# Search of sub-keys laid over 44 attention steps instead of 33, with a new buffer layout and later key and value loads

## The chip, the cores and the metric

One core of a Trainium2 chip runs the whole kernel. The time is the device time of one execution in microseconds (us). TensorE (PE in the profile) does the matrix products, ScalarE (ACT) the exponentials and the copies with a scale, VectorE (DVE) the searches for maxima and the element-wise work, GpSimd (POOL) the rest of the element-wise work, and SyncE (SP) issues the transfers.

## The reference

The block is an attention layer followed by a layer with 4096 experts, of which each token and head picks eight by product keys:

```python
h  = x + attention(layernorm(x))         # 2048 tokens, width 448, 16 heads of 28
q  = layernorm(h) @ w_q                  # per head two halves of 256
s1 = q1 @ k1.T;  s2 = q2 @ k2.T          # 64 sub-keys each
t1, i1 = top8(s1);  t2, i2 = top8(s2)    # the search of sub-keys
cand = t1[:, None] + t2[None, :]         # 64 pairs; the best 8 are experts 64*i1 + i2
g = softmax(top8(cand))
out = h + sum(g * gelu(x . u[expert]) * v[expert])
```

## The kernel before, in words

The order of the work on PE, DVE, ACT, POOL and SP is written out by hand: generators are merged by `weave`, which gives each generator a stretch of positions and always advances the one whose next position is lowest. One position is one step of the attention.

**Attention.** The 2048 queries are taken in 4 batches of 512, the 16 heads in 4 groups of 4, the 2048 keys in 16 tiles of 128: 256 steps, 16 per batch and group. Step `u` first issues `scores(u + 2)`: 12 matmuls into the PSUM tile `S` (L565) and two exponentials on ACT from `S` to `P` (L569). Then it issues `values(u)`: 4 matmuls in the program, 8 in the trace, from `P` and `V` into the PSUM tile `A` (L592). A step in the set `paired` issues `values(u + 1)` as well, so that the next step has none and leaves room for other matmuls. Each step needs two buffers of `S`, and there are three. When a group of 16 steps is over, DVE copies `A` to `o` (L597); two steps later `finish` transposes `o` into the PSUM tile `M` (L580), and DVE divides by the row sums (L582, L583).

**The tile M.** Everything else that PE does during the attention goes through `M`, of which there is a single buffer (`P[0]` has `bufs=1`). It is filled by `finish`, by `project` (four transposes, L122, then the product with `wo`, L93 with `woh` and `wol`), by the search (11 matmuls, L93 with `w` and `Xb`, emptied by ACT into `fresh`, L797), and by `places_of` (four transposes, L924, emptied by two ACT copies, L97). PE cannot fill `M` again before the engine that empties it has done so.

**Projection and search of a batch.** When the attention of a batch of 512 tokens is over, `project` runs in 26 steps from `begin[b]`: 73, 133 and 195. `search(b)` then goes through 16 items, one for each of four groups of heads (`i`) and four tiles of tokens (`j`), in the order (0,0) (0,1) (1,0) (1,1) (2,0) ... (3,1) (0,2) (0,3) ... Each item takes two of the 33 turns of the generator: one with the matmuls and `fresh`, one with the first half of the maxima on DVE (L816, L818); the second half goes with the next item. The weights of a head group are two tiles of 512 KB, the high and the low half (`w`, L784), in three buffers that they share. In the last item of a head group the four products with the low half stand first, in the others they stand last.

**Beside it** run the pairs of candidates (`pairs_of`, POOL and DVE), the scale of the expert tables (`tops`, DVE), their splitting (`part`, POOL), and for batches 0 and 1 the transposes of the chosen slots (`places_of`), from position 174 and 238 on. Batch 3 is projected after the attention. `load_kv` requests the keys and values of four steps (`kS` and `V`, 4 buffers each), and the values' request waits for the last use of the buffer that it overwrites.

In the text below a step is named by `u`; the steps 91 to 132, 151 to 194 and 213 to 255 are those in which the searches run after the change or before it.

Of the kernel before, what the change touches and what calls it, by code (L numbers as in the profile page):

```python
# [12 lines left out]
F16 = mybir.dt.float16  # L13
# [9 lines left out]
N, D, H, DH = 2048, 448, 16, 28  # L23
NT, NB = N // 128, N // 512
# [37 lines left out]
def block(ctx: ExitStack, tc: tile.TileContext, x, wqk, wv, wo, wq, k12, uT, v, cst, out):  # L62
# [131 lines left out]
    def chain(*gens):  # L194
        for g in gens:
            yield from g
# [3 lines left out]
    def flush():  # L200

        while due:
            due.pop(0)()
# [16 lines left out]
    def halves(dst, src, cols):  # L220

        nc.sync.dma_start(dst, src[:, :, cols].rearrange("f p n -> p f n"))
# [4 lines left out]
    def load_kv(n):  # L227

        if n < len(PIECES):
            _, g, c = PIECES[n]  # L230
            kS = lp.tile([128, 2, 512], F16, name="kS", bufs=4)
            halves(kS, ks_d[g], slice(512 * c, 512 * c + 512))
            V = lp.tile([128, 4, 4, 32], F32, name="V", bufs=4)
            nc.sync.dma_start(V.rearrange("p t h d -> p (t h d)"), v_d[g, c].rearrange("p t c -> p (t c)"))
            kv[n] = kS, V

    def load_q(n):

        if n < 4 * NB:
            b, g = divmod(n, 4)  # L240
            qs[n] = lp.tile([128, 2, 512], F16, name="qS")
            halves(qs[n], qs_d[g], slice(512 * b, 512 * b + 512))
# [309 lines left out]
    def attention(paired, behind_values):  # L552

        O = {}

        def scores(u):
            n, k = divmod(u, NT)
            if k == 1:
                load_q(n + 1)
            kS, qS = kv[u // 4][0], qs[n]  # L560
            S = [pss.tile([128, 2, 512], F32, name="S") for _ in range(2)]
            for m, (a, c) in enumerate(((0, 0), (0, 1), (1, 0))):
                for j in range(4):
                    r = slice(32 * j, 32 * j + 32)
                    nc.tensor.matmul(S[j // 2][:, j % 2], kS[r, a, 128 * (k % 4):128 * (k % 4) + 128], qS[r, c],  # L565
                                     start=m == 0, stop=m == 2)
            Pt = pp.tile([128, 4, 512], F32, name="P", bufs=3)
            for i in range(2):
                nc.scalar.activation(Pt[:, 2 * i:2 * i + 2], S[i], AF.Exp, scale=escale[:, n % 4:n % 4 + 1])  # L569
            return Pt  # L570

        def finish(n, o):

            b, g = divmod(n, 4)
            if g == 0:
                ob[b] = (w2 if b % 2 else pp).tile([128, 4, D], F32, name="ob", bufs=1)
            flush()
            pt = P[0].tile([128, 4, 4, 32], F32, name="M")
            for c in range(4):
                nc.tensor.transpose(pt[:, c].rearrange("p h d -> p (h d)"), o[:, 128 * c:128 * c + 128], ident)  # L580
            r = pp.tile([128, 4, 4], F32, name="r")
            nc.vector.reciprocal(r, pt[:, :, :, 28])  # L582
            nc.vector.tensor_tensor(ob[b][:, :, 112 * g:112 * g + 112].rearrange("p c (h d) -> p c h d", h=4),  # L583
                                    pt[:, :, :, :DH], r.unsqueeze(3).to_broadcast([128, 4, 4, DH]), op=OP.mult)

        def values(u, Pt):
            n, k = divmod(u, NT)
            if k == 0:
                O[n] = P[0].tile([128, 512], F32, name="A")
            V = kv[u // 4][1]  # L590
            for j in range(4):
                nc.tensor.matmul(O[n][32 * j:32 * j + 32], V[:, k % 4, j], Pt[:, j], start=k == 0, stop=k == NT - 1)  # L592
            if k % 4 == 3:
                load_kv(u // 4 + 4)
            if k == NT - 1:
                o = pp.tile([128, 512], F32, name="o", bufs=1)
                nc.vector.tensor_copy(o, O.pop(n))  # L597
                return o

        steps = 4 * NB * NT  # L600
        done = None

        def summed(u):
            nonlocal done
            o = values(u, Pts.pop(u))
            if o is not None:
                done = o

        Pts = {u: scores(u) for u in range(2)}
        for u in range(steps):  # L610
            if u + 2 < steps:
                Pts[u + 2] = scores(u + 2)
            flush()
            if u % NT == 2 and u > NT and u not in behind_values:
                finish(u // NT - 1, done)
            if u in Pts:
                summed(u)
            if u in paired:
                summed(u + 1)
            if u in behind_values:  # L620
                finish(u // NT - 1, done)
            yield
        finish(4 * NB - 1, done)
        yield
# [93 lines left out]
    PROJECT = 26  # L718
# [23 lines left out]
    def scores_of(XH, XL, w, j, turned=False):  # L742
        c = slice(128 * j, 128 * j + 128)
        flush()
        p = P[0].tile([128, 512], F32, name="M")
        n = 128 * w[0].shape[1]
        pairs = products(lambda t: XH[:, t, c], lambda t: XL[:, t, c], lambda t: w[0][:, :, t], lambda t: w[1][:, :, t])
        high, low = pairs[:4] + pairs[8:], pairs[4:8]
        mm_all(p[:, :n], low + high if turned else high + low)
        return p[:, :n]  # L750
# [23 lines left out]
    def search(b, order):  # L774


        loads = {}
        heads = [i for n, (i, j) in enumerate(order) if not n or order[n - 1][0] != i]

        def load(n, k):  # L780

            if n < len(heads):
                loads[n, k] = w = sp.tile([128, 4, 4, 128], F16, name="w", bufs=3)
                nc.sync.dma_start(w, wp_d[heads[n]][:, k])  # L784

        load(0, 0)
        load(0, 1)
        load(1, 0)
        yield
        last = None  # L790
        g = 0
        for n, (i, j) in enumerate(order):
            if last:
                best(*last)
            turned = n + 1 == len(order) or order[n + 1][0] != i
            src = sp.tile([128, 512], F32, name="fresh", bufs=2)
            nc.scalar.activation(src, scores_of(*X[b], (loads[g, 0], loads[g, 1]), j, turned), AF.Identity, scale=gscale[:, i:i + 1])  # L797
            if turned:
                load(g + 1, 1)
                load(g + 2, 0)  # L800
                g += 1
            yield
            best(2 * i, j, src[:, :256])
            last = 2 * i + 1, j, src[:, 256:]
            yield
        best(*last)
        yield

    SEARCH = 33
# [10 lines left out]
    def best(i, j, src):  # L820

        if i == 0:
            ti[j] = bk.tile([128, 2, 2 * H, 8], F32, name=f"ti{j}")
        t8, i8 = ti[j][:, 0], ti[j][:, 1].bitcast(U32)
        found([(t8[:, 4 * i + k], i8[:, 4 * i + k], src[:, 64 * k:64 * k + 64]) for k in range(4)])
# [104 lines left out]
    def places_of(b, eng):  # L930
        yield from soften()
        yield from to_slots(eng, b)
# [96 lines left out]
    sp = late.enter_context(tc.tile_pool(name="sp", bufs=2, side="right", reuse_waits="tile"))  # L1029
# [46 lines left out]
    FOLDED = 68  # L1076

    with tc.manual_schedule(engines={ET.PE, ET.DVE, ET.Activation, ET.Pool, ET.SP}):
        load_kv(2)
        load_kv(3)  # L1080
        begin = [FOLDED + 5, 67 + 66, 67 + 128]
        a = attention({4 * h for h in range(1, H)} | {t + k for t in begin for k in (1, 7, 13, 19)}
                      | {t + 25 + 2 * n for t in begin for n in range(16)},
                      {u for t in begin for u in range(t, t + 26) if u % NT == 2})
        weave((islice(a, FOLDED), FOLDED, 0, FOLDED), (fold[0].run(fold_p, P[0]), Fold.STEPS, 0, Fold.STEPS),
              *[(fold[0].parts(fold_p, i), Fold.PARTS, 16 * i + (18 if i < 3 else 16), 16 * i + 32 if i < 3 else FOLDED) for i in range(4)],
# [23 lines left out]
        work = [(a, 257 - FOLDED, 0, 257 - FOLDED), (load_wo(), 5, 0, 5)]  # L1110
        for b in range(3):
            t = begin[b] - FOLDED
            look = search(b, [(i, j) for g in ((0, 1), (2, 3)) for i in range(4) for j in g])
            work += [(project(b), PROJECT, t, t + PROJECT), (islice(look, 1), 1, t + 20, t + 21)]
            t += 26
            p = 64 * b + 174 - FOLDED
            work += [(look, SEARCH, t, t + SEARCH)]
            if b < 2:
                work += [(chain(*[pairs_of(j, nc.gpsimd) for j in range(4)]), 4 * PAIRS_POOL, t + 18, p),
                         (places_of(b, nc.scalar), PLACES, p, p + 2 * PLACES)]  # L1120
            else:
                work += [(pipeline([pairs_of(j, nc.gpsimd) for j in (0, 1)], 6), 6 + PAIRS_POOL, t + 20, 257 - FOLDED)]
# [132 lines left out]
    tag = ["A"]  # L1255
    ws = None
    for b in range(NB):
        n = AHEAD if b else UP0
# [4 lines left out]
        work = [(experts(b, n, acc), 32, 0, 1)]  # L1263
# [60 lines left out]
```

## Time and profile before

| | us |
|---|---|
| median of 3 runs | 1593.74 |
| the runs | 1595.08, 1593.74, 1589.76 |
| profiled execution, whole | 1590.46 |
| its span, first to last instruction | 1588.7 |
| PE busy | 1532.8 (96%) |
| DVE busy | 1146.5 (72%) |
| ACT busy | 910.0 (57%) |
| POOL busy | 362.1 (23%) |

The attention takes from 155 us to 831 us of the span. In that stretch ACT is busy for about 34 of each 40 us and PE for nearly all. The granted clock of PE is 0.997 over the span. A matmul that waits in the middle of a group for a buffer is drawn longer, not idle, so the busy share of PE says little here; the distance from one group of `S` to the next tells more.

### The profile page before, as it was taken

How to read it: one execution, taken by the hardware profiler on the slowest of the kernel's cores; microseconds unless marked ns; L12 is line 12 of the kernel's file. 1: busy time of each engine (PE TensorE's matmuls, PEld its weight loads, DVE VectorE, ACT ScalarE, POOL GpSimd, SP SyncE). 2: the span in 40 equal slices, each digit the busy share in tenths (PEclk: the TensorE clock that was granted, in tenths of full speed). 3: DMA queues.
4: the chain of work that ended last, by engine and by line, in shares of the span. 5: the costliest groups of instructions: out<-in, count | busy, mean ns of one | idle time of the engine just before them, and what ended most of it. 6: DMA issues, size and time to landing. Idle time of an engine off the chain costs nothing.

```text
span 1588.7 us, 33185 instructions
## 1 busy us (share of the span) xinstructions
PE 1532.8 (96%) x12540; PEld 669.4 (42%) x12540; DVE 1146.5 (72%) x3924; ACT 910.0 (57%) x1220; POOL 362.1 (23%) x488
## 2 busy tenths in 40 slices
PE   5999999999999999999998999999999999999999
PEld 3444222233333333333335654455445554555444
DVE  7763365444477867666599899789998999789623
ACT  3544888888888888888873433344423344334322
POOL 1242000534235743787662000000000000000000
PEclk9999999999999999999999999999999999999999
DMA  8424687556677756569733244453344534443444
GB/s 278 141 97 127 224 268 244 173 179 215 213 252 218 245 173 219 165 202 278 225 114 101 91 133 130 130 182 119 105 136 129 158 107 132 141 137 117 121 144 134
DMA packets 170018, 266.10 MB, mean 167 GB/s; under 512 B 25472, under 2 KB 102016, under 8 KB 169856
## 3 DMA queue, kind: packets, MB, share of 16 engines
q1 hardware_dynamic: 165632, 261.88, 52.9%
q10 hardware_dynamic: 4224, 2.10, 0.4%
q8 instruction: 98, 1.61, 0.4%
q14 instruction: 64, 0.52, 0.1%
HBM read 211.88 MB, written 49.28 MB: 164 GB/s over the span
## 4 chain that ended last, share of the span: by engine, by line
PE 74%; DVE 18%; DMA 2%; POOL 2%; issue 2%; ACT 1%; SPq 0%; DVEq 0%; POOLq 0%
PE M L93 14%; PE acc L1234 14%; PE A L592 13%; PE S L565 11%; PE A L93 9%; PE pq L93 6%; DVE p L994 4%; DVE fg L979 2%; DVE G L1015 2%; PE M L273 2%; PE A L1021 1%; DVE ring L1206 1%; DVE f L973 1%; DVE w L1209 1%; PE A L1011 1%
## 5 line engine op out<-in xcount | busy, mean ns | idle before, releaser
L569 ACT ACTIVATE P<-S,escale 128x1024 f32<-128x1024 f32 x512 | 535.7, 1118 | 82.1 <-PE S L565 75.9
L1234 PE MATMUL acc<-v,w 128*128 128x448 f16 x1536 | 308.3, 354 | 1.3 <-DVE w L1209 1.0
L592 PE MATMUL A<-P,V 128*32 128x512 f32 x2048 | 257.6, 601 | 1.3 <-DVE o L597 1.3
L565 PE MATMUL S<-qS,kS 32*128 32x512 f16 x3072 | 230.4, 378 | 2.9 <-ACT P L569 2.2
L1234 PEld LDWEIGHTS <-w 128*128 128x128 f16 x1536 | 148.4, 98 | 143.4 <-DVE w L1209 4.0
L93 PEld LDWEIGHTS <-u 128*128 128x128 f16 x1386 | 131.1, 98 | 146.4 <-issue 6.8
L93 PE MATMUL A<-Xb,u 128*128 128x512 f16 x759 | 178.6, 384 | 2.5 <-DVE G L1015 2.5
L1160 ACT ACTIVATE ring<-A,ugelu 128x512 f32<-128x512 f32 x71 | 48.7, 687 | 218.8 <-PE A L93 218.8
L994 DVE TENSOR_TENSOR p<-st,iota 128x2048 f16<-128x2048 f16 x128 | 156.7, 1225 | 14.9 <-PE M L1011 8.1
L93 PE MATMUL M<-w,Xb 128*128 128x512 f16 x704 | 163.1, 379 | 3.5 <-DVE oh L137 1.6
L1206 DVE SCALAR_TENSOR_TENSOR ring<-ring,wscale,G 128x512 f32<-128x512 f32 x128 | 92.1, 746 | 77.7 <-ACT ring L1160 77.6
L565 PEld LDWEIGHTS <-kS 32*128 32x128 f16 x3072 | 63.6, 92 | 198.3 <-issue 162.7
L93 PE MATMUL M<-Xb,u 128*128 128x512 f16 x627 | 146.4, 379 | 0.0
L93 PEld LDWEIGHTS <-Xb 128*128 128x128 f16 x704 | 64.0, 98 | 92.8 <-issue 20.5
L1208 ACT ACTIVATE w<-ring 128x512 f16<-128x512 f32 x128 | 75.8, 622 | 41.1 <-DVE ring L1206 28.9
L592 PEld LDWEIGHTS A<-P,V 128*32 128x32 f32 x2048 | 48.2, 108 | 120.5 <-issue 110.9
L816 DVE MAX8 ti<-fresh 128x8 f32<-128x64 f32 x384 | 57.3, 212 | 53.8 <-ACT fresh L797 53.6
L1051 POOL TENSOR_SCALAR raw<-raw,scale 128x512 f32<-128x512 f32 (+1 forms) x64 | 47.4, 741 | 188.7 <-PE M L158 145.8
L1209 DVE SCALAR_TENSOR_TENSOR w<-w,ring 128x512 f16<-128x512 f16 x128 | 84.9, 686 | 7.2 <-ACT w L1208 6.9
L1160 ACT ACTIVATE ring<-M,ugelu 128x512 f32<-128x512 f32 x57 | 39.2, 688 | 87.8 <-PE M L93 86.1
L979 DVE TENSOR_TENSOR fg<-f,st 128x2048 f16<-128x2048 f16 x64 | 78.8, 1231 | 0.1
L818 DVE FIND_INDEX8 ti<-ti,fresh 128x8 uint32<-128x64 f32 x384 | 76.9, 220 | 0.0
(197 smaller groups left out, 1897.3 us busy)
## 6 DMA issues: line engine op xcount, KB each, us to landing
v<-vs SPq DMA_DIRECT2D x128, 336.0 KB, 2.9
u<-us SPq DMA_DIRECT2D x126, 256.0 KB, 2.6
w<-wp SPq DMA_DIRECT2D x56, 512.0 KB, 4.9
kS<-ks SPq DMA_DIRECT2D x64, 256.0 KB, 4.9
V<-vd SPq DMA_DIRECT2D x64, 256.0 KB, 3.6
wr<-in_wq_dram SPq DMA_DIRECT2D x32, 448.0 KB, 4.2
vs<-hl SPq DMA_DIRECT2D x32, 336.0 KB, 5.2
seen<-in_uT_dram SPq DMA_DIRECT2D x32, 256.0 KB, 5.0
```

The costliest lines, as they stand in the source:

```text
L93: nc.tensor.matmul(ps, l, r, start=i == 0, stop=i == len(pairs) - 1)
L565: nc.tensor.matmul(S[j // 2][:, j % 2], kS[r, a, 128 * (k % 4):128 * (k % 4) + 128], qS[r, c], start=m == 0, stop=m == 2)
L569: nc.scalar.activation(Pt[:, 2 * i:2 * i + 2], S[i], AF.Exp, scale=escale[:, n % 4:n % 4 + 1])
L592: nc.tensor.matmul(O[n][32 * j:32 * j + 32], V[:, k % 4, j], Pt[:, j], start=k == 0, stop=k == NT - 1)
L818: nc.vector.max_index(i, t, src)
L979: nc.vector.tensor_tensor(fg.rearrange("p t k f u -> p t k (f u)"), f1.rearrange("p t f u -> p t (f u)").unsqueeze(2).to_broadcast([128, T ...
L994: newest[0] = nc.vector.tensor_tensor(p1, pairs(0, s, TG, 128), ids(TG, 128), op=OP.is_equal).ins
L1160: gelu[0] = nc.scalar.activation(act, p, AF.Gelu_apprx_tanh, scale=ugelu).ins
L1206: nc.vector.scalar_tensor_tensor(av, av, wscale, of_expert(b, f), op0=OP.mult, op1=OP.mult)
L1208: nc.scalar.activation(w[:, 0], a, AF.Copy, scale=1.0 / LS)
L1209: newest[0] = nc.vector.scalar_tensor_tensor(w[:, 1], w[:, 0], -LS, a, op0=OP.mult, op1=OP.add).ins
L1234: nc.tensor.matmul(acc[j][:, :D], l, r, start=f == 0 and k == 0, stop=f == 31 and k == 2)
```

## The change

It does four things. The search of a batch is laid over the positions from `begin + 19` to `begin + 63` (214 to 257 for the last batch), where it ran from `begin + 26` to `begin + 59`; its first loads are requested at `begin + 14`, not `begin + 20`. The set `paired` is worked out from the positions of the items, a step before each, and leaves out the last step of a group of 16. The low half of the weights gets one buffer of its own, and the high half keeps two. `load_kv` is called two steps later, when the buffer has been free for two steps, for the same piece.

```diff
@@ values
-            if k % 4 == 3:
-                load_kv(u // 4 + 4)
+            if k % 4 == 1 and u > 4:
+                load_kv(u // 4 + 3)
@@ search, load
-                loads[n, k] = w = sp.tile([128, 4, 4, 128], F16, name="w", bufs=3)
+                loads[n, k] = w = sp.tile([128, 4, 4, 128], F16, name="w", tag="w" + "hl"[k], bufs=2 - k)
@@ block
-        a = attention({4 * h for h in range(1, H)} | {t + k for t in begin for k in (1, 7, 13, 19)}
-                      | {t + 25 + 2 * n for t in begin for n in range(16)},
+        searched = [(t + 19, min(t + 63, 257)) for t in begin]
+        spots = [4 * h + 1.5 for h in range(1, H)]
+        spots += [t + k + 0.5 for t in begin for k in (2, 8, 14, 20)]
+        spots += [lo + (2 * n + 0.5) * (hi - lo) / SEARCH for lo, hi in searched for n in range(16)]
+        paired = {int(s - 0.5) - 1 for s in spots}
+        a = attention({u for u in paired if u % NT < NT - 1},
                       {u for t in begin for u in range(t, t + 26) if u % NT == 2})
...
-            work += [(project(b), PROJECT, t, t + PROJECT), (islice(look, 1), 1, t + 20, t + 21)]
+            work += [(project(b), PROJECT, t, t + PROJECT), (islice(look, 1), 1, t + 14, t + 15),
+                     (look, SEARCH, searched[b][0] - FOLDED, searched[b][1] - FOLDED)]
...
-            work += [(look, SEARCH, t, t + SEARCH)]
```

What stands beside the slots' transposes of batch 0 on ACT, steps 183 to 189, before the change (`P` is the exponentials of a step, two of them; `fresh` empties `M` after an item of the search, L97 empties it after the transposes):

```order
L797 ACTIVATE fresh<-M,gscale 128x512
L569 ACTIVATE P<-S,escale 128x1024 x2
L97 ACTIVATE st<-M 128x2x128
L97 ACTIVATE st<-M 128x256
L569 ACTIVATE P<-S,escale 128x1024 x2
L797 ACTIVATE fresh<-M,gscale 128x512
L569 ACTIVATE P<-S,escale 128x1024 x2
```

And with the change, the same place on ACT:

```order
L797 ACTIVATE fresh<-M,gscale 128x512
L569 ACTIVATE P<-S,escale 128x1024 x6
L797 ACTIVATE fresh<-M,gscale 128x512
L97 ACTIVATE st<-M 128x2x128
L97 ACTIVATE st<-M 128x256
L569 ACTIVATE P<-S,escale 128x1024 x4
L97 ACTIVATE st<-M 128x2x128
L97 ACTIVATE st<-M 128x256
L797 ACTIVATE fresh<-M,gscale 128x512
```

Before, a step's exponentials stood between any two instructions that empty `M`; now an item of the search and a set of transposes follow each other within one step, in step 184 the item first, in step 186 the transposes first. The same two meetings are found in steps 248 and 250. Three steps (`x6`) often lie between two items, where there were two.

On PE, the `finish` of step 162 before the change (`A<-P,V` are the values of two steps; the next item of the search stands behind the following step's 12 matmuls into `S`):

```order
L565 LDWEIGHTS kS
L565 MATMUL S<-qS,kS 128x512
L580 MATMUL M<-ct,o 128x128 x4
L592 MATMUL A<-P,V 32x512 x8
L565 LDWEIGHTS kS
```

And with the change:

```order
L565 LDWEIGHTS kS
L565 MATMUL S<-qS,kS 128x512
L580 MATMUL M<-ct,o 128x128 x4
L93 LDWEIGHTS Xb
L93 MATMUL M<-w,Xb 128x512
```

The item of the search now follows the transposes of `finish` directly, with no matmul of another tile in between; the same is found in steps 178 and 242.

## The prediction

> **What bounds the kernel now.** I read the page first, then the busy time by stretch, then PE's timeline step by step, then the waits. The page gives the span, the busy shares and the chain that ended last:
>
> ```profile
> span 1588.7 us, 33185 instructions
> PE 1532.8 (96%) x12540; PEld 669.4 (42%) x12540; DVE 1146.5 (72%) x3924; ACT 910.0 (57%) x1220; POOL 362.1 (23%) x488
> ...
> PE 74%; DVE 18%; DMA 2%; POOL 2%; issue 2%; ACT 1%; SPq 0%; DVEq 0%; POOLq 0%
> ```
>
> The busy time in the stretches that the change touches (steps 91 to 132, 151 to 194, 213 to 252; columns: us, then busy time of PE, PE's weight loads, DVE, ACT, POOL, then granted clock, DMA share, GB/s):
>
> ```profile
> 376.63:494.68 118.05, 117.71 (x1048) 37.90 (x1045) 68.46 (x473) 99.38 (x101) 47.34 (x60) 1.00 0.69 226
> 539.91:663.84 123.93, 123.47 (x1104) 40.03 (x1101) 85.13 (x563) 106.88 (x115) 67.86 (x94) 1.00 0.63 200
> 708.29:824.42 116.13, 114.62 (x1015) 37.34 (x1012) 79.92 (x551) 97.31 (x103) 74.90 (x103) 1.00 0.68 212
> ```
>
> PE is the bound, yet "busy" hides waits. PE's timeline during a search, one pair of steps:
>
> ```profile
> 447.44 0.83 PE L565 MATMUL S<-qS,kS 32*128 32x512 f16 x12
> 448.19 1.92 PE L592 MATMUL A<-P,V 128*32 128x512 f32 x16
> 450.05 0.83 PE L565 MATMUL S<-qS,kS 32*128 32x512 f16 x12
> 450.81 2.55 PE L93 MATMUL M<-w,Xb 128*128 128x512 f16 x11
> 453.29 0.83 PE L565 MATMUL S<-qS,kS 32*128 32x512 f16 x12
> ```
>
> From start to start, S costs 0.76, two values 1.86, an item of the search 2.48: 5.85 for the pair, nothing waits. Beside it the steps just ahead of the first search, which hold S and one value each:
>
> ```profile
> 385.03 0.83 PE L565 MATMUL S<-qS,kS 32*128 32x512 f16 x12
> 385.79 1.07 PE L592 MATMUL A<-P,V 128*32 128x512 f32 x8
> 386.79 1.15 PE L565 MATMUL S<-qS,kS 32*128 32x512 f16 x12
> 387.87 1.06 PE L592 MATMUL A<-P,V 128*32 128x512 f32 x8
> 388.87 1.08 PE L565 MATMUL S<-qS,kS 32*128 32x512 f16 x12
> 390.88 1.08 PE L565 MATMUL S<-qS,kS 32*128 32x512 f16 x12
> ```
>
> The first such "lone" step takes 1.76 (0.76 + 1.00), the next 2.08, then 2.01: S is drawn 1.15 and 1.08 long, not 0.83. The cause is the third buffer of S: the second half of a step's S goes into the buffer that the first exponential of the step before empties. So after a lone step the next S loses 0.33 (2.08 - 1.75), in a row 0.25. That is what a wider spread could win back: PE's slack in lone steps.
>
> **Work on PE.** Matmuls are neither added nor removed. By the order of the changed program values stand in 87 groups in these stretches, not 75, and two apart cost 2.00 where a pair cost 1.86: 12 x 0.14 = **+1.7**.
>
> **Lone steps.** Before, 16 S groups in the three stretches follow a lone step: 155, 192, 217 and two in the first search at 0.33 for the first of a row (95, 132), eleven at 0.25: 1.6 + 2.8 = 4.4. With the change an item comes every 2.67 steps, so most items have one lone step behind them, and its successor pays even though PE is full around it: 27 first ones and 3 in a row, 8.9 + 0.8 = 9.7. Step 133 no longer follows lone ones: -0.25. Net **+5.0**. The exponentials do not become the bound: three steps with an item cost ACT 3 x 2.01 + 0.69 = 6.7, PE 1.76 + 2.61 + 3.24 = 7.6.
>
> **Waits on M.** ACT and PE around the transposes of the slots (emptied in L97):
>
> ```profile
> 635.09 2.12 ACT L569 ACTIVATE P<-S,escale 128x1024 f32<-128x1024 f32 x2
> 637.22 0.66 ACT L97 ACTIVATE st<-M 128x256 f16<-128x256 f16 x2
> ```
>
> ```profile
> 634.17 0.83 PE L565 MATMUL S<-qS,kS 32*128 32x512 f16 x12
> 634.93 1.92 PE L592 MATMUL A<-P,V 128*32 128x512 f32 x16
> 636.78 0.40 PE L924 MATMUL M<-ident,sl 128*128 128x128 f16 x4
> 637.11 0.83 PE L565 MATMUL S<-qS,kS 32*128 32x512 f16 x12
> 637.93 2.53 PE L93 MATMUL M<-w,Xb 128*128 128x512 f16 x11
> ```
>
> The end of an item, PE's next S, and ACT's emptying of M:
>
> ```profile
> 562.27 0.38 PE L93 MATMUL M<-w,Xb 128*128 128x512 f16 x1
> ...
> 562.58 0.40 PE L565 MATMUL S<-qS,kS 32*128 32x512 f16 x4
> 562.69 0.69 ACT L797 ACTIVATE fresh<-M,gscale 128x512 f32<-128x512 f32 x1 [0.35 <-PE M L93]
> ```
>
> PE at the end of the attention, where transposes stand right behind a finish:
>
> ```profile
> 827.36 1.68 PE L592 MATMUL A<-P,V 128*32 128x512 f32 x8
> ...
> 829.93 0.63 PE L580 MATMUL M<-ct,o 128*128 128x128 f32 x4 [0.52 <-DVE o L597]
> 831.57 0.44 PE L122 MATMUL M<-ct,ob 128*128 128x128 f32 x2 [1.01 <-DVE ob L583]
> ```
>
> Steps 186 and 250 become S, transposes, item. ACT takes the exponentials first: they start 0.92 after S (635.09 - 634.17) and L97 ends 3.71 after it (637.88). The item could start 1.09 after S (0.76 + 0.33) and starts at 3.76: 2.67 each, since the two values that filled this time are no longer there: 5.3. Steps 184 and 248 become S, item, transposes: fresh ends 0.80 after the item, so 0.86 each: 1.7. Steps 162, 178 and 242 become S, finish, item; the row at 831.57 prices a user of M right behind a finish at 1.01, DVE being free: 3.1. Sum **+10.1**. Behind the waiting item stand the next S and, with it, ACT: nothing overtakes.
>
> **Smaller meetings.** In steps 94, 154 and 216 an item stands one S (0.76) behind the product with wo, which takes DVE about 0.86 to fetch (like fresh): 0.1 each. In 92, 152 and 214 an item stands 1.76 behind the transposes that DVE halves into oh and ol. DVE's queue there holds pieces of 1.28, such as one half of an item's maxima and their places:
>
> ```profile
> 825.43 0.59 DVE L816 MAX8 ti<-fresh 128x8 f32<-128x64 f32 x4
> ...
> 826.71 0.58 DVE L816 MAX8 ti<-fresh 128x8 f32<-128x64 f32 x4
> ```
>
> Between 0 (DVE free) and 3 x 1.28 I take 0.3, since the order puts such a piece ahead in one place at most. Together **+0.6**.
>
> **What the change removes.** Waits of PE and of SP in the attention, the wait in step 99, and the transfers' times:
>
> ```profile
> PE M L93 <- DMA w<-wp: 1.5, 2, 1.3
> ...
> PE A L592 <- DVE o L597: 1.3, 1, 1.3
> ```
>
> ```profile
> SPq L234 <- PE A L592: 146.1, 55, 6.1
> ```
>
> ```profile
> 397.47 2.54 PE L93 MATMUL M<-w,Xb 128*128 128x512 f16 x11 [0.30 <-PE S L565]
> ```
>
> ```profile
> w<-wp SPq DMA_DIRECT2D x56, 512.0 KB, 4.9
> kS<-ks SPq DMA_DIRECT2D x64, 256.0 KB, 4.9
> ```
>
> The low weights were late twice, 1.5 in all. Now the request goes out after the fourth matmul of the last item of a group, seven matmuls (7/11 of 2.48 = 1.6) sooner, and where three steps lie between items there is more room still; at the closest (two steps), from release to need lie 1.6 + 2.61 + 0.76 + 1.6 = 6.5, against 4.9 from issue to landing: **-1.5**. In step 98 the finish now stands further ahead of the item: **-0.3**. The later keys and values cost nothing: a piece is first read nine steps after its request, at least 9 x 1.75 = 15.8 against 4.9. SP's 146 us of waiting for values go, but in the attention PE waits for no transfer except w; worth 0, and the DVE wait for o (1.3) stays, since its step is untouched.
>
> **The end of the attention.** The last item moves to step 253. The last values were drawn 1.68 long there, not 1.07, waiting about 0.5 for the last exponentials; now the item fills that; but the last half of the maxima now stands on DVE between the copy of A and the last division: 1.3 long, by the rows above it ends about 0.6 after the finish. Net **+0.1**.
>
> **The sum:** 1.7 + 5.0 + 10.1 + 0.6 - 1.5 - 0.3 + 0.1 = **+15.7 us**. The profiled execution took 1590.46 as a whole, 1.76 more than its span; it is the second fastest of the four times known, whose mean is 1592.3, and the median of the runs shown is 1593.74. Against the mean, 1592.3 + 15.7 = **1608 us** (1606.2 against the profiled one alone).
>
> The Trainium skill ("Trainium Kernel Development and Optimization", Best Practices) says to double-buffer so that transfers overlap with compute; the low weights go against it with one buffer. By that rule the low weights would be exposed at each reload; no wait here shows that, and 6.5 against 4.9 speaks against it; the second rival below is this case, priced from rows.
>
> **Rivals.** First, DVE queues: in the second and third stretch DVE is busy 69% of the time, in pieces up to 1.3. A finish whose division finds one ahead waits that much more (3 x 1.3), and at seven ends of a group (111, 127, 159, 175, 191, 223, 239) the copy of A now has only one S to hide behind, where the row above shows 1.3 for such a meeting (7 x 0.9 beyond the 0.33 already counted). If half of them meet, +5, if all, +10: 1613 to 1618. DVE's share speaks for some of it; that the order issues the copy of A ahead of the item's maxima at most of these places speaks against much.
>
> Second, low weights late: where two steps lie between items (6 times), a landing 1.3 later than the gap costs 6 x 1.3 = 8: 1616. It decides from a landing above 6.5 us.
>
> Third, lone steps are free: if the exponentials had caught up by then, the S behind an isolated lone step would not wait. Then the 9.7 falls away: 1608 - 9.7 = 1598. Against it: 386.79 follows just such a step.
>
> Fourth, not slower: the waits on M fall where PE would have waited anyway, because ACT, with one item in 2.67 steps rather than in 2, runs so far ahead that M and S are always free. Without the 10.1 and the 9.7 it is 15.7 - 19.8 = -4.1: 1588. It decides at step 186: the item would have to start about 1.1 us after that step's S, not 3.8. Against it stands that ACT empties M behind exponentials that cannot begin before the S of the same step; for it, only that ACT is busy no more than 84 to 86% of the stretches.
>
> **How the numbers follow.** Chances: the sum as it stands 0.53; DVE queues 0.15; weights late 0.05; lone steps free 0.13; not slower 0.14. 0.3% (4.8 us) is about what a measurement of this kernel can tell from no change. The third case ends at +6, so a third of it is within 0.3%; the fourth at -4.1, half of it within, half faster. Slower 0.53 + 0.15 + 0.05 + 0.09 = 0.82, same 0.04 + 0.07 = 0.11, faster 0.07. The runs shown spread by 2.7 to either side. The range reaches from below the third case, 1596, to the first at its worst, 1618; it leaves out the fourth case and a little at each end.
>
> **What the profile after would show.** S groups of 1.1 us behind lone steps about 30 times in the three stretches; items of the search that wait for ACT's L97 by 2.7 twice, transposes that wait for fresh by 0.9 twice, items that wait for DVE's division by 1.0 three times; no PE wait for w; SP's wait for the values gone; the three stretches longer by about 1, 9 and 5 (the third with the end of the attention). The prediction is wrong if the first stretch, which holds no meeting on M, gets clearly shorter, if the second is not longer by at least 5, or if PE's waits on M show up with ACT still running its exponentials without a gap.

## The result

| | before | changed | ratio, 95% interval |
|---|---|---|---|
| median of 4 runs, us | 1593.05 | 1606.72 | 1.0087 (1.0065 to 1.0109) |
| profiled execution, us | 1590.46 | 1606.85 | |
| its span, us | 1588.7 | 1605.0 | |

The change makes the kernel slower by 13.7 us; 1608 was predicted. The page of the changed kernel shows little of it: the busy time of PE is 8.6 us longer, the granted clock over the span is 0.993 instead of 0.997, and the chain is as it was.

```profile
span 1605.0 us, 33183 instructions
PE 1541.4 (96%) x12540; PEld 670.2 (42%) x12540; DVE 1144.0 (71%) x3924; ACT 907.9 (57%) x1220; POOL 357.9 (22%) x488
...
PE 75%; DVE 19%; DMA 2%; issue 1%; ACT 1%; POOL 1%; SPq 0%; DVEq 0%; POOLq 0%; ACTq 0%
```

The busy time by stretch (columns as before) shows where it is: the same three stretches, from the first S of steps 91, 151 and 213 to the first S of steps 133, 195 and 253, take 118.87, 133.42 and 121.46 us, where they took 118.05, 123.93 and 116.13.

```profile
376.78:495.65 118.87, 118.83 (x1048) 37.93 (x1045) 66.55 (x463) 99.72 (x101) 47.31 (x60) 1.00 0.68 219
542.60:676.02 133.42, 127.72 (x1105) 40.55 (x1103) 83.38 (x549) 105.97 (x115) 68.86 (x98) 0.99 0.58 178
720.41:841.87 121.46, 117.19 (x1013) 37.26 (x1010) 83.44 (x560) 96.53 (x102) 81.60 (x114) 0.99 0.60 189
```

In the second and third PE's busy time is now 5.7 and 4.3 us short of the stretch, and the granted clock is no longer 1.00. PE's waits during the attention (in all, how often, the longest) name the gaps:

```profile
PE M L93 <- ACT st L97: 5.0, 2, 2.5
PE M L93 <- DVE ob L583: 3.0, 3, 1.0
PE M L580 <- DVE oh L137: 2.3, 1, 2.3
...
PE M L924 <- ACT fresh L797: 1.6, 2, 0.8
PE A L592 <- DVE o L597: 1.2, 1, 1.2
```

The waits of an item for L97, twice 2.5, for the division in `finish`, three times 1.0, and of the transposes for `fresh`, twice 0.8, are the seven meetings on M (two users of the one buffer side by side). No wait for `w` is left. PE's timeline has steps 184 (639.66) and 186 (646.67) in full:

```profile
639.66 0.83 PE L565 MATMUL S<-qS,kS 32*128 32x512 f16 x12
640.42 2.55 PE L93 MATMUL M<-w,Xb 128*128 128x512 f16 x11
643.74 0.38 PE L924 MATMUL M<-ident,sl 128*128 128x128 f16 x4 [0.78 <-ACT fresh L797]
...
646.67 0.83 PE L565 MATMUL S<-qS,kS 32*128 32x512 f16 x12
647.43 0.40 PE L924 MATMUL M<-ident,sl 128*128 128x128 f16 x4
650.31 3.63 PE L93 MATMUL M<-w,Xb 128*128 128x512 f16 x11 [2.48 <-ACT st L97]
653.88 1.36 PE L565 MATMUL S<-qS,kS 32*128 32x512 f16 x12
```

and ACT's the reason, the exponentials of the same step ahead of the copy that empties M:

```profile
647.59 2.12 ACT L569 ACTIVATE P<-S,escale 128x1024 f32<-128x1024 f32 x2 [0.49 <-PE S L565]
649.60 0.66 ACT L97 ACTIVATE st<-M 128x256 f16<-128x256 f16 x2
```

One thing was not foreseen: the item behind the wait is drawn 3.63 long, not 2.55, and the next S 1.36, not 0.83. The clock (the last column but two) tells why. The three stretches below are the wait, the item and the step after it; from 651.59 to 655.00 the granted clock is 0.50, and such a stretch is called a spell of half clock below:

```profile
646.67:650.31 3.64, 1.16 (x20) 0.54 (x17) 0.00 (x0) 3.10 (x5) 3.49 (x6) 1.00 0.00 0
650.31:653.88 3.57, 3.57 (x12) 1.20 (x12) 0.00 (x0) 0.00 (x0) 3.41 (x4) 0.68 0.37 109
653.88:656.16 2.28, 2.28 (x21) 0.45 (x20) 1.46 (x14) 1.51 (x2) 2.13 (x4) 0.75 0.54 174
```

### The profile page after: what moved, and what is told of

It is laid out like the page before. It is cut to its first block, busy times and chain, and to the rows that moved or that the text cites. A ratio compares the mean times of both kernels' runs of the same rounds, so it can differ in the third digit from the quotient of the medians.

```text
span 1605.0 us, 33183 instructions
## 1 busy us (share of the span) xinstructions
PE 1541.4 (96%) x12540; PEld 670.2 (42%) x12540; DVE 1144.0 (71%) x3924; ACT 907.9 (57%) x1220; POOL 357.9 (22%) x488
## 4 chain that ended last, share of the span: by engine, by line
PE 75%; DVE 19%; DMA 2%; issue 1%; ACT 1%; POOL 1%; SPq 0%; DVEq 0%; POOLq 0%; ACTq 0%
PE M L93 15%; PE A L592 14%; PE acc L1238 13%; PE S L565 12%; PE A L93 8%; PE pq L93 6%; DVE p L994 4%; DVE G L1015 2%; DVE fg L979 2%; PE M L273 2%; DVE ring L1210 2%; DVE w L1213 1%; PE A L1021 1%; DVE f L973 1%; DVE pos L818 1%
## 5 line engine op out<-in xcount | busy, mean ns | idle before, releaser
L565 PE MATMUL S<-qS,kS 32*128 32x512 f16 x3072 | 236.9, 381 | 2.9 <-ACT P L569 2.2
L93 PE MATMUL A<-Xb,u 128*128 128x512 f16 x759 | 175.3, 379 | 2.4 <-DVE G L1015 2.4
```

What stands on the lines that cost most here:

```text
L93: nc.tensor.matmul(ps, l, r, start=i == 0, stop=i == len(pairs) - 1)
```

## The experiments

Theory: the seven meetings on M (9.6 us of waits) and the lone steps (about 5) make the change slow, and the clock falls behind the longest waits. Rivals: the buffers and the transfers cost the time; DVE's queues do; the waits on M are covered. Each ratio is against the kernel before, measured in the same series.

| | kernel | median, us | ratio, 95% interval |
|---|---|---|---|
| e1 | change, but search on 33 steps | 1588.49 | 0.9977 (0.9963 to 0.9990) |
| e2 | change, but old requests of keys and values | 1608.97 | 1.0100 (1.0084 to 1.0115) |
| e3 | change, but three shared buffers for `w` | 1607.71 | 1.0085 (1.0071 to 1.0099) |
| e4 | change, seven items moved off the meetings | 1596.17 | 1.0021 (1.0012 to 1.0030) |
| e5 | before, keys and values two steps later | 1587.16 | 0.9962 (0.9950 to 0.9974) |
| e6 | e4, 19 items with two matmuls put back | 1594.56 | 1.0009 (0.9998 to 1.0020) |
| e7 | before, with five meetings on M | 1617.34 | 1.0161 (1.0144 to 1.0178) |
| e8 | before, low weights in their own buffer | 1593.04 | 1.0007 (0.9993 to 1.0021) |
| e9 | before, keys and values four steps later | 1588.17 | 0.9966 (0.9954 to 0.9978) |
| e10 | e6 with 14 of the 19 places | 1593.21 | 0.9996 (0.9985 to 1.0007) |

### e1: the spread undone, the rest kept

```diff
-        paired = {int(s - 0.5) - 1 for s in spots}
+        a = attention({4 * h for h in range(1, H)} | {t + k for t in begin for k in (1, 7, 13, 19)}
+                      | {t + 25 + 2 * n for t in begin for n in range(16)},
...
-                     (look, SEARCH, searched[b][0] - FOLDED, searched[b][1] - FOLDED)]
+            work += [(look, SEARCH, t, t + SEARCH)]
```

> The search is laid over 33 steps again, with the paired steps of the kernel before; the buffer of the low weights and the later keys and values stay. Theory (the meetings on M and the lone steps cost the time): both are gone, so the time is that of the kernel before less the waits for w, about 1.5 us: 1590 to 1593, some 14 us below the changed kernel. Rival (the buffers or the transfers cost it): it stays near 1603 to 1607. In the profile: no wait of PE for w, no wait of an item for L97 of 2.5 us.

1588.49: the slowness is the spread's. Steps 91 to 132 and 151 to 194 take what they took before to 0.01 us, and steps 213 to 252 1.76 less, the waits for `w`. It came out below the range given (1590 to 1593); the runs of the request, below, explain a part of that.

### e2 and e3: requests and buffers undone, each alone

```diff
-            if k % 4 == 1 and u > 4:
-                load_kv(u // 4 + 3)
+            if k % 4 == 3:
+                load_kv(u // 4 + 4)
```

> Only the time at which keys and values are requested is put back; the search stays on 44 steps. Theory: worth nothing, 1605 to 1608 as the changed kernel; SP's queue waits for the values as long as in the kernel before (146 us instead of 84.5), and PE for none of it. Rival (SP's order moves the loads of w or of keys): 3 us or more to either side.

```diff
-                loads[n, k] = w = sp.tile([128, 4, 4, 128], F16, name="w", tag="w" + "hl"[k], bufs=2 - k)
+                loads[n, k] = w = sp.tile([128, 4, 4, 128], F16, name="w", bufs=3)
```

> The weights of the search share three buffers again; the search stays on 44 steps. Theory: the waits of PE for w come back, but with 2.67 steps to an item they are shorter than the 1.5 us of the kernel before: 1606 to 1609 (0 to +2 against the changed kernel). Rival (low weights with one buffer arrive late and cost time): 3 to 8 us below the changed kernel, 1599 to 1604.

Neither brings the kernel below 1604: the rival is out. But e2, at 1608.97, is a little above the range, and its trace has the waits at step 75 (4.36 us instead of 3.22) and for `w` (1.1) again, while e3, with the shared buffers, has none for `w`, though they were expected back. So the request, which was costed at nothing, seemed to be what takes the waits away, and the buffer, to which that was put down, seemed to do nothing. e5 and e8 test that.

### e5, e8 and e9: the parts on the kernel before

e5 and e9 change the request alone (two and four steps later), e8 the buffer alone.

```diff
-            if k % 4 == 3:
-                load_kv(u // 4 + 4)
+            if k % 4 == 1 and u > 4:      # e5; in e9 k % 4 == 3
+                load_kv(u // 4 + 3)
```

> The kernel before with one part of the change: keys and values are requested two steps later. Theory A, new from the first experiments (SP's queue, no longer held up by the values, lets the weights of the projection and of the search go out earlier): the 1.3 us at step 75 and the 1.5 us of waits for w both go, 1.0 to 3.5 us below the kernel before, about as the variant on 33 steps with all the rest of the change. Rival B (as predicted: the request is worth 0, the buffer of the low weights takes away the waits for w): within 1 us of the kernel before, waits for w still there.

> The kernel before with one part of the change: the low weights in a buffer of their own. Theory A (the requests of keys and values hold the queue): the waits for w stay at 1 to 2 us and the time is within 1 us of the kernel before. Rival B (the buffer takes the waits away): 1.5 us less and no wait for w in the trace.

> The kernel before with the keys and values requested four steps later instead of two (and nothing else). A piece is then first read seven steps after its request, at least 7 x 1.75 = 12.2 us against a landing of 4.9. Theory (once the queue is ahead of the weights' need, more delay buys nothing): the same as with two steps, 1585 to 1589, no wait for w and none at step 75. Rival (each two steps buy as much again, or a piece comes late): 3 us or more to either side of 1587.

Theory A holds for `w`; at step 75 the way is another one, shown below. The request alone makes the kernel faster, by 0.38% (5.9 us, where 1.0 to 3.5 were expected), with both waits gone; the buffer alone changes nothing and leaves 2.0 us of waits for `w`. Four steps are no better than two: the waits for `w` are gone, but step 75 takes 4.15, so that this part of the expectation failed. In e9 SP waits for the values' buffer 5.5 us in all, in one place, and in e5 61.3; that e9 is no faster speaks against a price of SP's wait by itself. SP's queue shows what has a price. In the kernel before, at step 237 (`kS`, `V` and `w` are the requests of keys, values and weights):

```profile
764.42 0.37 SPq L222 DMA_DIRECT2D kS<-ks  x1
769.51 0.32 SPq L234 DMA_DIRECT2D V<-vd  x1
...
772.16 1.07 SPq L784 DMA_DIRECT2D w<-wp  x2
```

```profile
775.99 1.69 PE L93 MATMUL M<-w,Xb 128*128 128x512 f16 x7
778.99 1.02 PE L93 MATMUL M<-w,Xb 128*128 128x512 f16 x4 [1.31 <-DMA w<-wp]
```

SP stands at the values from 764.8 to 769.5 for their buffer; behind it other requests and then `w` go out, at 772.16, and the four products with the low half wait for them until 778.99. In e5:

```profile
769.99 1.83 SPq L784 DMA_DIRECT2D w<-wp  x2
771.87 0.43 SPq L222 DMA_DIRECT2D kS<-ks  x1
772.35 0.46 SPq L234 DMA_DIRECT2D V<-vd  x1
```

```profile
774.77 2.55 PE L93 MATMUL M<-w,Xb 128*128 128x512 f16 x11
```

The weights now go first, and the values no longer wait. Against the item's start (775.99 and 774.77) the request stands 0.95 us earlier, 4.78 ahead of it and not 3.83. The two requests of `w` also land 5.4 and 5.9 us after their issue, where it was 6.8 and 7.4. Keys and values now stand behind them and not ahead of them; that this makes them land sooner is not shown.

At step 75 it is the order of the requests that differs. The weights of the projection (`wor`) come in through SP too, and DVE, which rounds them, had not got to splitting `oh`. Before:

```profile
337.47 0.40 DVE L631 CAST woh<-wor 128x448 fp32r<-128x448 f32 x1 [3.10 <-DMA wor<-in_wo_dram]
```

```profile
339.49 1.09 PE L93 MATMUL M<-woh,oh 128*128 128x448 f32 x4 [1.21 <-DVE oh L137]
```

SP does not stand at the values there, but keys and values go out between the third and the fourth request of `wor`; in e5 these two go out together:

```profile
331.42 0.33 SPq L635 DMA_DIRECT2D wor<-in_wo_dram  x1
331.85 0.39 SPq L222 DMA_DIRECT2D kS<-ks  x1
332.32 0.42 SPq L234 DMA_DIRECT2D V<-vd  x1
332.89 0.33 SPq L635 DMA_DIRECT2D wor<-in_wo_dram  x1
```

```profile
330.55 2.18 SPq L635 DMA_DIRECT2D wor<-in_wo_dram  x2
```

In e5 the last rounding starts at 334.89 instead of 337.47, and step 75 is 1.28 us shorter. The same order goes with the same time in all twelve traces: in the seven with the request two steps later step 75 takes 3.19 to 3.22, in the five where keys and values stand in between, e9 among them, 3.62 to 4.50. The two places make 3.1 of the 4.0 us between the two profiled executions; the medians lie 5.9 apart, and the rest was not traced.

### e4: the meetings taken away

Each moved item also moves the step that does two values ahead of it.

```diff
+                turns[2 * n] += {162: 1, 178: 1, 242: 1, 184: -1, 248: -1, 186: 1, 250: 1}.get(u, 0)
+                turns[2 * n + 1] = max(turns[2 * n + 1], turns[2 * n] + 0.3)
```

> The search stays on 44 steps, but seven of its items are moved by one step (162 to 163, 178 to 179, 242 to 243, 184 to 183, 248 to 247, 186 to 187, 250 to 251), so that none stands beside a finish or beside the transposes of the slots. Theory: the seven waits on M, 5.0 + 3.0 + 1.6 = 9.6 us in the trace, go, and with the two long ones the two spells of half clock behind them (about 1.3 us each): 1594 to 1597. The 2 to 3 us above the kernel before that are left belong to lone steps (+5), work (+1.7) and the waits for w (-1.5) and what the changed order won elsewhere. Rival (the time is lost to lone steps and to DVE's queues, and a wait on M is covered by later work): 1602 to 1607.

1596.17, 10.6 us below the changed kernel: the theory's range. All seven waits are gone from the trace, and nothing has come in their place but 1.3 us of PE waiting for exponentials:

```profile
PE S L565 <- ACT P L569: 3.5, 8, 1.0
PE M L580 <- DVE oh L137: 2.2, 1, 2.2
PE M L122 <- DVE ob L583: 1.4, 1, 1.4
PE A L592 <- DVE o L597: 1.3, 1, 1.3
```

The three stretches are 0.83, 2.82 and -0.11 longer than before, not 0.82, 9.49 and 5.33: the first holds no meeting and did not move.

### e7: the meetings alone, on the kernel before

```diff
-            work += [(look, SEARCH, t, t + SEARCH)]
+            work += [(look, SEARCH, t + 0.1, t + 0.1 + SEARCH)]
-                         (places_of(b, nc.scalar), PLACES, p, p + 2 * PLACES)]
+                         (places_of(b, nc.scalar), PLACES, p + 0.5, p + 0.5 + 2 * PLACES)]
```

> The kernel before, on 33 steps, with the transposes of the slots moved half a step, so that in steps 185, 187, 189, 249 and 251 they stand directly ahead of an item of the search, behind a step's S; nothing else changes. Theory (a meeting on M is priced at 2.5 to 2.67 us by the exponentials that ACT takes first, wherever it falls): 5 x 2.5 = 12.5, and where the wait lies inside one window of the clock gate another 1.2 each: 12 to 18 us above the kernel before, 1605 to 1611. Rival (the time of the change comes from the spread, the meeting is partly covered): under 6 us above, below 1599.

The transposes are moved by half a position and the search by a tenth, so that the transposes stand directly ahead of an item. The kernel is 24 us slower, more than the theory gave. The five waits have the size that was expected:

```profile
PE M L93 <- ACT st L97: 12.4, 5, 2.5
PE M L93 <- DMA w<-wp: 3.2, 2, 2.7
```

Steps 185 and 187 are alike up to the item, and then not:

```profile
638.72 0.40 PE L924 MATMUL M<-ident,sl 128*128 128x128 f16 x4
641.60 2.53 PE L93 MATMUL M<-w,Xb 128*128 128x512 f16 x11 [2.48 <-ACT st L97]
...
647.44 0.40 PE L924 MATMUL M<-ident,sl 128*128 128x128 f16 x4
650.32 4.22 PE L93 MATMUL M<-w,Xb 128*128 128x512 f16 x11 [2.48 <-ACT st L97]
```

The step takes 6.11 in the first case (and the same in step 249), 7.79 in the second (and in 189; 7.71 in 251), against 3.28 before; the 0.33 of the transposes comes off the step ahead. So the wait costs 2.50, and a spell of half clock behind it 1.6 to 1.7 more, in three of five places. Together that is 5 x 2.5 + 5.0 = 17.5 in these steps. The rest: the waits for `w` are 1.7 longer than before, a clock spell in step 147 costs 1.6 (the wait ahead of it is there before too), and some 5 come behind the attention, which has three more windows of half clock at its start; these were not taken apart.

### e6 and e10: the lone steps

Two of an item's eleven matmuls are put behind the values of the lone step that follows, which makes that step longer than an exponential pair needs.

```diff
+            head = len(pairs) - 2 if n in behind_step else len(pairs)
+            for z, (l, r) in enumerate(pairs):
+                if z == head:
+                    yield
+                nc.tensor.matmul(m, l, r, start=z == 0, stop=z == len(pairs) - 1)
```

> The variant on 44 steps without meetings on M, and in 19 places where a lone step follows an item directly the last two of the item's eleven matmuls (0.45 us) stand behind that lone step's values. Theory (the S behind a lone step waits 0.33 us for the exponential that frees its second half, whatever PE has to do): the 0.33 goes 19 times, -6.3 us against the variant without meetings, about 1590; S groups behind lone steps are drawn 0.83, not 1.15. Rival (the 0.33 is no loss: the exponentials lag by as much and the next S waits instead, or M, held over one S more, costs new waits): 1594 to 1600.

> The variant that puts the last two matmuls of an item behind the following lone step's values, in 14 of the 19 places: those whose next step but one starts with a finish, or whose lone steps stand in a row, are left whole. Theory (each place wins the 0.33 of the S behind it and loses 0.11 by the cut of the item, and the rest of the 19's gain went into waits of finish for M): 14 x 0.22 = 3.1 us less than the variant without meetings in the three stretches, 1591 to 1594. Rival (the gain comes back as a wait elsewhere in any case): 1595 to 1597.

Step 95 on PE, in the changed kernel and then in e6 (where added lines shift the numbers: S is L566, the values L593, the item L809):

```profile
391.93 0.83 PE L565 MATMUL S<-qS,kS 32*128 32x512 f16 x12
392.69 1.07 PE L592 MATMUL A<-P,V 128*32 128x512 f32 x8
393.69 1.15 PE L565 MATMUL S<-qS,kS 32*128 32x512 f16 x12
```

```profile
392.99 0.82 PE L566 MATMUL S<-qS,kS 32*128 32x512 f16 x12
393.75 1.06 PE L593 MATMUL A<-P,V 128*32 128x512 f32 x8
394.74 0.61 PE L809 MATMUL M<-w,Xb 128*128 128x512 f16 x2
395.28 0.83 PE L566 MATMUL S<-qS,kS 32*128 32x512 f16 x12
```

S behind the lone step is 0.83 long again in all 19 places, and where the step that it opens holds S and two values alone (13 of them) that step takes 2.61 instead of 2.94: the 0.33 is real. But the cut item costs 0.11 (2.81 + 2.29 against 3.24 + 1.75), so a place wins 0.22, and e6 won only 1.6 us, which is in the rival's range. In steps 178, 194 and 226 `finish` comes next and waits for `fresh`, 0.6 each, a new meeting on M; at 240, among lone steps in a row, 0.62 went the same way. e10 leaves those places whole and takes 1593.21, 3.0 below e4 as expected (14 x 0.22 = 3.1; 2.7 in the three stretches of the traces). It equals the kernel before, but with the later request in it; e5, with the request alone, beats it.

## Why the prediction was right, and where it was not

The total was right, 1608 against 1606.72, and its two main terms were. It was helped by errors that cancelled, which is luck. Us in the profiled executions, before against changed (16.3 apart, where the medians are 13.7 apart; executions of one kernel lie up to 5 us from each other, so the small rows hold for these two executions alone):

| step of the prediction | predicted | measured |
|---|---|---|
| work on PE (values apart) | +1.7 | +1.7 (87 groups against 75) |
| lone steps | +5.0 | +5.4 |
| waits on M | +10.1 | +9.7 |
| smaller meetings | +0.6 | 0 |
| waits for `w` | -1.5 | -1.8 |
| step 99 | -0.3 | -0.3 |
| clock behind the two long waits | none | +3.1 |
| step 75, wait for `oh` | none | -1.3 |
| steps 133 to 150 | in the lone steps | +1.7 |
| end of the attention, rest of the stretches | +0.1 | -0.7 |
| ahead of step 68 and behind the attention | 0 | -1.2 |

**Waits on M.** Steps 186 and 250 lose 2.55 each (predicted 2.67), 184 and 248 0.83 (0.86), 162, 178 and 242 0.99 (1.01). The rival that saw them covered fails at its own point: the item of step 186 starts 3.64 us after S, not 1.1. e4 and e7 show the cause from both sides.

**Lone steps.** In the three stretches 34 groups of S are drawn longer than 0.95, 19 before; what they lose rises from 5.6 to 11.2, of which 0.2 at step 187 is clock. e6 shows that the loss goes when the step is filled. The third rival, lone steps free, is out. The prediction's 0.33 is too small for step 192, where S is drawn 1.63 long before and 1.62 after, which cancels.

**The step that failed: "worth 0".** SP's wait for the values was costed at nothing, since PE waits for no transfer but `w`. But that wait was what made `w` late: in SP's queue `w` stood behind a request that waited for its buffer (764.8 to 769.5 above). The -1.5 came out right, but for the wrong reason: the buffer of the low weights, which the prediction credits, does nothing alone (e8) and is not needed on 44 steps (e3). And SP's wait did not go; it fell by two fifths, from 146.1 in 55 places:

```profile
SPq L234 <- PE A L592: 84.5, 37, 6.9
```

The second rival, low weights late, is out: PE has no wait for `w`. It was to decide from a landing above 6.5 us, and in the first stretch of the changed kernel the slowest request of `w` took 7.3; the 4.9 of the prediction is a median. The Trainium skill ("Trainium Kernel Development and Optimization", Best Practices) advises double buffers, so that transfers overlap with compute. No reload was exposed here for want of a second buffer: the low weights' own single buffer or a share of three made no difference once the request was later (1606.72 against 1607.71 on 44 steps, 1588.49 against 1587.16 on 33).

**The clock.** The prediction took the granted clock as given (0.997). The spells behind steps 186 and 250 add 3.1: 1.6 in steps 186 and 187, 1.5 in 250.

**Steps 133 to 150** hold a `finish` (146) that waited 2.25 for DVE's split of `oh`, 1.46 before; in the changed kernel DVE had stood 0.88 for a value of POOL. A spell of half clock behind it adds the rest.

**DVE queues**, the first rival, cost next to nothing: the wait of values for `o` is 1.2 us in one place, as before, and the last division comes 0.4 later. The stretches came out as forecast, about 1, 9 and 5: 0.8, 9.5, and 6.8 for the third with the end of the attention.

## What to carry to other kernels

Price a reordering by the buffers with one copy that it brings two users of side by side: spreading work more evenly cost here 0.8 to 2.55 us at each such meeting, whatever the engines' busy shares. A wait on a queue that nobody seems to need was free here only where nothing needed stood behind it in that queue; moving one request by two steps saved 5.9 us here, while the rest of the change cost time. And a wait of TensorE can cost more than its length: 1.6 to 1.7 us of half clock stood behind some of the waits of 2.5.

## What the runs showed of the hardware

The granted clock is recorded in windows of 3.413 us on a fixed grid. Over the twelve profiled executions, from the first record of the clock (20 to 25 us) on, the time that PE idles within a window was set against the clock of the next. Of windows with 1.99 us or more of idling, 30 of 30 were followed by one at half clock; with 1.6 to 1.99, 12 of 35; with 1.0 to 1.6, 15 of 115; with 0.6 to 1.0, 1 of 110. The same wait of 2.48 us is thus free of it when it lies across two windows (step 185 of e7, where the half-clock windows put a border at 640.56, inside the wait) and dear when it lies inside one (step 187, 647.39 to 650.80). Where the grid falls differs from execution to execution. Whether that makes the spread of the times is not shown, but the clock goes with it: over 114 executions (the changed kernel, the ten variants and the last series of the kernel before), each kernel's mean taken out, the span is 1.1 us longer for each 0.001 less of clock (correlation -0.77), and one spell is 0.001 of the span.

The Trainium skill ("TensorE: Matmul & The Clock Gate", What's actually happening) gives the same window, 3413 ns and free-running, and names an idle window of about 3.4 us as what halves the clock. The traces agree on the window; here 2.0 us of idling within it were enough.
